# Exponentials turned by DMAs inside SBUF, and decay tiles spread from a table by VectorE, in a fused decay-attention and feed-forward kernel

## Chip, cores and metric

The kernel runs on one core of a Trainium2 chip. The metric is device time in microseconds of one execution; before the change it is 1072.73 us (median of 3 runs, 1070.98 to 1072.88). A core has TensorE (PE in the profile; its weight loads are PEld), VectorE (DVE), ScalarE (ACT), GpSimd (POOL) and SyncE (SP), which here issues nearly all DMAs. SBUF is the on-chip memory of 128 partitions, PSUM the matmul output with eight banks of 512 fp32 columns.

## The reference

For 8 batches of 8 heads, 576 positions and 64 dimensions, causal attention with a decay; its output, 4608 tokens of 512 features, goes through a feed-forward with a leaky slope per hidden unit.

```python
scores = scale * np.matmul(q, k.transpose(0, 1, 3, 2))
log_f = np.log(np.clip(f, 0.0001, 1.0))
cum = np.cumsum(log_f, axis=-1)
decay = cum[:, :, :, None] - cum[:, :, None, :]
causal = np.triu(np.ones((S, S), dtype=bool), k=1)
scores = np.where(causal, -1000000000.0, scores + decay)
scores = scores - np.max(scores, axis=-1, keepdims=True)
attn = np.exp(scores)
attn = attn / (np.sum(attn, axis=-1, keepdims=True) + 1e-09)
attn_out = np.matmul(attn, v)
...
h = x @ w_in
g = np.maximum(h, 0.0) + alpha * np.minimum(h, 0.0)
out = g @ w_out
```

The decay of the query's own position is the same for a whole row and drops out with the maximum, so only the keys' `cum` has to be added to the scores.

## The kernel before

**Work.** Two heads make a pair; pair n (0 to 31) is batch n // 4. `attention(n)` does one pair, `ffn1(b)` the first feed-forward product of batch b for 16 blocks of hidden units (`ffn1(8)` takes the last 64 positions of all batches), `ffn2(u)` the second one for a unit of 256 tokens. The first product stores its hidden values in DRAM (`hd`, line 807) and the second loads them again, as seven products of sums.

**Order.** Nothing is run in program order. Every step is an `op` of class `Plan` with an engine, an estimated duration, a key (smaller goes first), the steps that it depends on, and the buffers of `Ring`s that it holds. `Plan.run` simulates the engines and emits on each engine's queue the step that can start first, the smaller key among equals. DMAs go through one modelled channel (line 160). Attention of pair n has keys around 10 n, `ffn1` keys from 1e6, so the feed-forward fills what the attention leaves of TensorE. Each engine then works through its queue in order, and waits where something is not ready.

**One pair.** `load_n` (line 425) loads q and k (433, 434) and, from pair 4 on, splits each in two parts (ScalarE 472, GpSimd 473). It makes the decay tiles `Z` (two heads, all 128 partitions hold the same row of -8 cum) and `Zt` (for the tail): for pair 0 by a small matmul, for the others by DMAs from the DRAM row `c8`, broadcast to the partitions (443, 463). GpSimd adds the causal mask to their blocks (447 to 449, 464). The 576 queries are four tiles of 128 and a tail of 64 per head; the tail's two heads share 128 partitions. For each tile TensorE makes the scores (`stretch`, `tail`), VectorE adds the decay and takes the minimum (639, 541), and ScalarE takes the exponential in SBUF (508; tiles `es` and `e`).

P·V needs the exponentials with keys in the partitions. So TensorE transposes each block of 128 x 128 (`blocks`, 521; 677 for the last 64 keys of the tail), and ScalarE copies them from PSUM (517, tiles `eT`). For the fourth tile (i = 3) of pairs from `NX[0]` = 8 on another way is taken: the tile goes to DRAM (`ex`, 659), comes back in blocks of 32 partitions (`em`, 660), and VectorE transposes blocks of 32 x 32 (665). A reordered copy of v (`vs`, 497) goes with it. P·V (`prods_of`) is emitted with the third tile's scores of the next pair (`values`, `behind`); both heads run side by side on 64 columns each.

`quotients` and `fetch` bring the row sums through DRAM to a broadcast tile `ri` (598). `rest` multiplies (721) and splits the result into x (723, 725), in a ring of seven buffers, one per pair, which `ffn1` of that batch frees.

**Beside it.** `split64` (306 to 329) loads each of 16 blocks of `w_in` as 64-bit floats into two buffers `wr` (313) and turns them into two fp32 parts `wi` on ScalarE, VectorE and GpSimd; a work tile `wa` goes with it. `ffn1` takes a PSUM bank of ring `rH` for a block, twelve matmuls of 512 columns fill it (793), ScalarE and VectorE take it out (800 to 806) into one of four buffers `hs`. When the attention is done, its SBUF is given to the weights and buffers of `ffn2`.

Some lines that the steps go by:

```python
PC = ((0, 256), (256, S))
...
o_c8 = op("SP", 400, lambda: sy.dma_start(c8, ft()), -49, o_8, [bft], kb=147)
...
rx = Ring(Store([xx[:, 1024 * i : 1024 * i + 1024].rearrange("p (k q) -> p k q", k=2) for i in range(7)]))
...
for tiles in ((0, 1), (2,), (3,)) if n < NE else ((0, 1, 3), (2,)):
```

Of the kernel before, what the change touches and what calls it, by code (L numbers as in the profile page):

```python
# [29 lines left out]
NX = (8, B * NP)  # L30
# [53 lines left out]
class Plan:  # L84
# [30 lines left out]
    def run(self):  # L115
# [7 lines left out]
        while left:  # L123
# [63 lines left out]
def attention_moe(  # L187
    ctx: ExitStack,
    tc: tile.TileContext,
    qq: bass.AP,  # L190
    kk: bass.AP,
    vv: bass.AP,
    vs: bass.AP,
# [20 lines left out]
    ex = [dram.tile([2, 128, 512], F32, name=f"ex{i}") for i in range(2)]  # L214
# [32 lines left out]
    rrq = ring(sp, 2, [128, QW], F32, "rq")  # L247
    rrk = ring(sp, 2, [128, S], F32, "rk")
    rZ = Ring(Store([(sp.tile([128, 2, ZW], F32, name=f"Z{i}"), sp.tile([128, S], F32, name=f"Zt{i}")) for i in range(2)]))
    rvr = ring(sp, 2, [128, 5, 2, D], F32, "vr")  # L250
# [13 lines left out]
    rwr = ring(sp, 2, [128, 512], U64, "wr")  # L264
    rwa = ring(sp, 1, [128, 512], U32, "wa")
# [7 lines left out]
    wbf = sp.tile([128, 512], BF16, name="wbf")  # L273
    sel = sp.tile([9, 6, 128], F32, name="sel")
# [150 lines left out]
    def load_n(n, held):  # L425
# [4 lines left out]
        bq, bk, bZ = Buf(rrq), Buf(rrk), Buf(rZ)  # L430
        kq = -99 if first else -59 if n == 1 else kl
        dq = [] if first else [o_scan]
        l_q = op("SP", 450, lambda: sy.dma_start(bq.t, qq[b, p]), kq, dq, [bq], kb=320)
        l_k = op("SP", 450, lambda: sy.dma_start(bk.t, kk[b, p]), kq, dq, [bk], kb=288)
        Z, Zt = (lambda: bZ.t[0]), (lambda: bZ.t[1])
        rz = []
        for h in range(2):
            if first:
# [12 lines left out]
        if first:  # L451
# [13 lines left out]
        if n < NN:  # L465
            held += [bq, bk]
            return [l_q, l_k], rz, rt, bZ, [(lambda: bq.t, lambda: bk.t)]
# [3 lines left out]
        for hi, lo, raw, ld, w in ((Qh, Ql, bq, l_q, QW), (Kh, Kl, bk, l_k, S)):  # L471
            o1 = op("ACT", c_acs(w), lambda hi=hi, raw=raw: ac.activation(hi(), raw.t, AF.Copy), kc, [ld], [raw, bQ])  # L472
            o2 = op("POOL", c_po(w), lambda hi=hi, lo=lo, raw=raw: po.tensor_tensor(lo(), raw.t, hi().bitcast(F32), ALU.subtract), kc, [o1], [raw, bQ])  # L473
            out += [o1, o2]
# [3 lines left out]
    waiting, behind, later_x = [], [], []  # L478

    def attention(n):  # L480
# [9 lines left out]
        bv = Buf(rvr)  # L490
        l_v = op("SP", 400, lambda: sy.dma_start(bv.t, vv[b, p]), kl + 1, [o_scan], [bv], kb=320)
        nt_ = 3 if n >= NN else 4
        bT1, bT2 = [Buf(rT1) for _ in range(2)], [Buf(rT2) for _ in range(2)]
        b3, bT3, turned = Buf(re3), Buf(rT3), NX[0] <= n < NX[1]
        if turned:
            bm, bvs = Buf(rm3), Buf(rvs)
            l_s = op("SP", 400, lambda: sy.dma_start(bvs.t, vs[b, p]), kl + 12, [o_scan], [bvs], kb=256)
# [27 lines left out]

        def tail(st):

            bt = Buf(re)
            prev = None
            for g in range(2):  # L530
# [9 lines left out]
                def red(bS=bS, ks=ks, g=g):  # L540
                    ve.tensor_tensor_reduce(out=bt.t[:, ks], in0=bS.t[:, :288], in1=bZ.t[1][:, ks],  # L541
                                            scale=-0.125, scalar=lo()[:, 9:10] if g else 3.0e38, op0=ALU.add, op1=ALU.min,
                                            accum_out=lo()[:, 4:5] if g else lo()[:, 9:10])
# [16 lines left out]
        def quick(bR, r_, key):  # L560
# [11 lines left out]
            q_ = op("PE", 1400, prods, key, [r_, o_sel], bB + [bR])  # L572
            for c0, c1 in ((0, 512), (512, S)):
# [30 lines left out]
        def stretch(tiles, st):  # L604
# [16 lines left out]
            s_0.append(s)  # L621
            done(s)
# [4 lines left out]
        def tile(h, i, st, bS, s, c0):  # L627
# [4 lines left out]
            at = (lambda t: t[:, h]) if i == 3 else (lambda t: t)  # L632
# [21 lines left out]
            if i == 3 and turned:  # L654
                if h == 0:
                    return
                d = ex[n % 2]
                key = k0 + 7.8
                o_ = op("SP", 400, lambda: sy.dma_start(d.rearrange("h q k -> q h k"), b3.t), key, [be[0][3][1], nm], [b3], kb=512)
                got = [op("SP", 400, lambda k=k: sy.dma_start(  # L660
                    bm.t[32 * k : 32 * k + 32], d[:, :, 128 * k : 128 * k + 128].rearrange("h (a c) s -> c (h a) s", c=32)),
                    key + 0.1, [o_], [bm], kb=128) for k in range(4)]
                for h_ in range(2):
                    def turn(h_=h_):
                        ve.transpose(bT3.t[:, h_].rearrange("p s (a c) -> p a s c", a=4),
                                     bm.t[:, 4 * h_ : 4 * h_ + 4].rearrange("p a (s r) -> p a s r", r=32))

                    e3.append(op("DVE", c_tr(512), turn, k0 + 13.5, got, [bm, bT3]))
                return
            if i >= 2:  # L670
# [3 lines left out]
                def tr2():  # L674
                    blocks(bT.t, 0, at(b1.t), range(i + 1))
                    if last:
                        pe.transpose(bT.t[0:64, 384:512], bt.t[:, 512:S], ident)  # L677

                t = op("PE", (i + 1 + last) * 109, tr2, st + 0.3, [nm, o_id] + ([nt] if last else []), [bT, b1] + ([bt] if last else []))
                to, tb = ((lambda: bT3.t[:, h]), bT3) if i == 3 else ((lambda: bT2[h].t[:, 0 : i + 1, 0:128]), bT2[h])  # L680
# [6 lines left out]
        def prods_of(r, out):  # L687

            def pv():
                both = []  # L690
                o = out()
                for h in range(2):
                    e1_, e2_ = bT1[h].t, bT2[h].t
                    if r == 0:
                        both.append([(0, 0, 256, e1_[:, 0:256]), (1, 128, 256, e1_[:, 256:384])])
                    else:
                        both.append([(j, 0, 128, e2_[:, j, 0:128]) for j in range(3)]
# [118 lines left out]
    for fc in range(NF):  # L816
        load_w_in(fc)
# [294 lines left out]
```

## Time and profile before

| What | Value |
| --- | --- |
| Time, median of 3 runs | 1072.73 us |
| Profiled execution: device time, span of the trace | 1073.41 us, 1071.6 us |
| Mean granted TensorE clock | 0.992 |
| DMA traffic | 202.15 MB, 189 GB/s |
| First feed-forward product, 1728 matmuls of 512 columns | 428.4 us busy on TensorE |
| Decay tiles by DMA (443, 463) | 62 loads of 256 KB, 62 of 144 KB |
| Round trip of the fourth tile (659, 660) | 24 stores of 512 KB, 96 loads of 128 KB |

The profile is one execution, recorded by the hardware. In a row of a group stand the line, the engine, the operation, the tile written and the tiles read, the shapes and the count; behind the bar the busy time in all and the mean of one in ns; then the engine's idle time just before and what ended it. In the timeline a row starts with its start and its length, both in us. "Busy" of TensorE counts matmuls from issue to the end that the profile models, and these overlap, so rows that follow each other closely are timed by the distance of their starts.

### The profile page before, as it was taken

The page shows a single profiled execution, that of the slowest core. Times are in us where ns is not written, and L with a number is a line of the kernel's source. Part 1 is how long each engine was busy: PE and PEld are TensorE (multiplying, and loading weights), DVE is VectorE, ACT ScalarE, POOL GpSimd, SP SyncE. Part 2 cuts the span into 40 slices and gives each one's busy share as a digit, 9 for nine tenths or more (in the row PEclk, how much of TensorE's full clock was granted, in tenths as well). Part 3 has the DMA queues.
Part 4 walks back from the last instruction along what each step waited for, and adds up shares of the span by engine and source line. Part 5 has one row for each costly group of instructions (what it writes and reads, how often), then busy time and mean ns, then how long its engine had stood idle before and what let it go on. Part 6 is the DMA issues. An engine that isn't in the chain of part 4 may idle for free.

```text
span 1071.6 us, 22543 instructions
## 1 busy us (share of the span) xinstructions
PE 1054.9 (98%) x8132; PEld 916.7 (86%) x8132; DVE 738.6 (69%) x1680; ACT 675.0 (63%) x1590; POOL 280.5 (26%) x407
## 2 busy tenths in 40 slices
PE   8889989999999999999999999999999999999998
PEld 5678867888888888888788888899999999999998
DVE  6788864555544545545544599779988898989994
ACT  6879877786766766667655375656454554646551
POOL 6578574553433434344221000000000000000000
PEclk9989999999999999999999999999999999999999
DMA  6967778987887986886763666464444443444411
GB/s 181 268 194 235 225 217 232 271 264 238 253 237 214 259 241 203 242 247 212 215 198 129 204 214 225 167 199 139 136 126 132 137 137 120 138 130 126 140 60 40
DMA packets 152441, 202.15 MB, mean 189 GB/s; under 512 B 18930, under 2 KB 89481, under 8 KB 152329
## 3 DMA queue, kind: packets, MB, share of 16 engines
q1 hardware_dynamic: 152041, 200.51, 61.3%
q8 instruction: 64, 1.05, 0.4%
q14 instruction: 48, 0.39, 0.1%
q10 hardware_dynamic: 288, 0.20, 0.1%
HBM read 139.55 MB, written 61.11 MB: 187 GB/s over the span
## 4 chain that ended last, share of the span: by engine, by line
PE 92%; DMA 2%; POOL 2%; DVE 1%; issue 1%; ACT 1%; SPq 0%; DVEq 0%; POOLq 0%
PE bank L332 86%; PE bank L521 5%; DMA Z<-c 2%; PE bank L392 1%; POOL Z L447 1%; DMA wr<-in_w_in_dram 0%; POOL wi L328 0%; POOL Z L448 0%; PE bank L677 0%; DVE eT L516 0%; DVE wa L322 0%; POOL Z L449 0%; ACT e L508 0%; POOL Ql L473 0%; POOL Kl L473 0%
## 5 line engine op out<-in xcount | busy, mean ns | idle before, releaser
L332 PE MATMUL bank<-xx,wi 128*128 128x512 f32 x1728 | 428.4, 397 | 2.3 <-ACT wi L327 1.8
L332 PEld LDWEIGHTS bank<-xx,wi 128*128 128x128 f32 x1728 | 314.4, 188 | 68.7 <-issue 4.8
L805 DVE SCALAR_TENSOR_TENSOR hs<-bank,sa,hs 128x512 f32<-128x512 f32 x96 | 71.2, 743 | 109.9 <-ACT hs L803 109.8
L332 PE MATMUL bank<-wot,xx 128*128 128x256 f32 x1008 | 123.9, 283 | 0.0
L332 PE MATMUL bank<-wi,xx 128*128 128x256 f32 x1008 | 123.9, 283 | 0.0
L332 PEld LDWEIGHTS bank<-wot,xx 128*128 128x128 f32 x1008 | 122.3, 192 | 0.0
L332 PEld LDWEIGHTS bank<-wi,xx 128*128 128x128 f32 x1008 | 122.3, 192 | 0.0
L508 ACT ACTIVATE e<-e,st 128x512 f32<-128x512 f32 (+2 forms) x160 | 109.2, 685 | 4.2 <-DVE st L541 2.0
L803 ACT ACTIVATE hs<-bank,ab 128x512 f32<-128x512 f32 x96 | 66.0, 688 | 63.4 <-PE bank L332 62.6
L517 ACT ACTIVATE eT<-bank 128x384 f32<-128x384 f32 (+2 forms) x192 | 83.3, 461 | 34.7 <-PE bank L332 20.1
L725 POOL TENSOR_TENSOR xx<-xs,xx 128x256 fp32r<-128x256 f32 x64 | 49.0, 783 | 136.6 <-ACT xx L723 136.4
L473 POOL TENSOR_TENSOR Ql<-rq,Qh 128x640 fp32r<-128x640 f32 x28 | 45.1, 1611 | 137.8 <-ACT Qh L472 89.7
L332 PE MATMUL bank<-eT,vr 128*64 128x128 f32 (+2 forms) x1408 | 80.0, 263 | 0.2 <-DVE eT L516 0.2
L332 PEld LDWEIGHTS bank<-eT,vr 128*64 128x64 f32 x1408 | 63.9, 138 | 14.1 <-issue 7.1
L447 POOL TENSOR_TENSOR Z<-Z,tri 128x384 f32<-128x384 f32 x64 | 60.0, 945 | 45.5 <-DMA Z<-c 31.2
L999 ACT ACTIVATE xx<-gx 128x1024 fp32r<-128x1024 f32 x48 | 50.8, 1058 | 30.8 <-PE bank L332 15.1
L521 PEld LDWEIGHTS bank<-ident,e 128*128 128x128 f32 x384 | 46.9, 146 | 20.5 <-issue 5.3
L521 PE MATMUL bank<-ident,e 128*128 128x128 f32 x384 | 62.2, 287 | 1.9 <-DVE st L639 1.6
L1002 DVE TENSOR_TENSOR xx<-gx,xx 128x1024 fp32r<-128x1024 f32 x48 | 58.6, 1220 | 7.4 <-ACT xx L999 7.4
L332 PE MATMUL bank<-wi,gh 128*128 128x256 f32 x504 | 62.4, 283 | 0.0
L332 PE MATMUL bank<-wot,gh 128*128 128x256 f32 x504 | 62.4, 283 | 0.0
L332 PEld LDWEIGHTS bank<-wot,gh 128*128 128x128 f32 x504 | 61.4, 192 | 0.1
(140 smaller groups left out, 1777.6 us busy)
## 6 DMA issues: line engine op xcount, KB each, us to landing
hd<-hs SPq DMA_DIRECT2D x144, 256.0 KB
wx<-hd SPq DMA_DIRECT2D x47, 512.0 KB
Z<-c SPq DMA_DIRECT2D x62, 256.0 KB
hr<-hd SPq DMA_DIRECT2D x25, 512.0 KB
ex<-e SPq DMA_DIRECT2D x24, 512.0 KB
em<-ex SPq DMA_DIRECT2D x96, 128.0 KB
rq<-in_qq_dram SPq DMA_DIRECT2D x32, 320.0 KB
vr<-in_vv_dram SPq DMA_DIRECT2D x32, 320.0 KB
```

Of the source, the lines that this page charges most:

```text
L332: pe.matmul(o, lhsT, rhs, start=start, stop=stop)
L392: op("PE", 800, lambda: [pe.matmul(bw.t, wbf[:, 0:128], wbf, start=True, stop=True) for _ in range(3)], -200, [o_wbf], [bw])
L447: m1 = op("POOL", c_po(128 * 3), lambda z4=z4: po.tensor_tensor(z4()[:, 6:9], z4()[:, 0:3], tb(3), ALU.add), kc + 0.1, got + [o_mask], [bZ])
L473: o2 = op("POOL", c_po(w), lambda hi=hi, lo=lo, raw=raw: po.tensor_tensor(lo(), raw.t, hi().bitcast(F32), ALU.subtract), kc, [o1], [raw, bQ])
L508: ex = op("ACT", c_exp(w), lambda: ac.activation(at(bt.t)[:, :w], at(bt.t)[:, :w], AF.Exp, bias=lo()[:, col : col + 1], scale=-1.0, accum_ ...
L517: return op("ACT", c_act(w), lambda: ac.activation(dst(), src(), AF.Copy), key, deps, [bank] + bufs)
L521: pe.transpose(t[:, c : c + 128], src[:, 128 * j : 128 * j + 128], ident)
L725: xl = op("POOL", c_po(256), lambda r=r, t0=t0: po.tensor_tensor(bx.t[:, 1, t0 : t0 + 256], bxs[r].t[:, 0:256], bx.t[:, 0, t0 : t0 + 256]. ...
L803: cp = op("ACT", c_act(512), lambda bh=bh, bs=bs, fc=fc: ac.activation(bs.t, bh.t, AF.Relu, scale=ab[:, fc : fc + 1]), -1000, [last, o_sg] ...
L805: cp = op("DVE", c_dve(512), lambda bh=bh, bs=bs, fc=fc: ve.scalar_tensor_tensor(bs.t, bh.t, sa[:, fc : fc + 1], bs.t, ALU.mult, ALU.add), ...
L999: his.append(op("ACT", c_acs(128 * GW * (j1 - j0)), lambda j0=j0, j1=j1, src=src, o_=o_: ac.activation(o_(0, j0, j1), src(), AF.Copy), key ...
L1002: rdy.append(op("DVE", c_dve(128 * GW * (j1 - j0)), lambda j0=j0, j1=j1, src=src, o_=o_: ve.tensor_tensor(o_(1, j0, j1), src(), o_(0, j0, ...
```

## The change

Seven things change together.

- From pair 9 on (`NX[0]` 9 instead of 8) the fourth tile's and now also the tail's exponentials are moved by 16 DMAs straight from SBUF to SBUF (32 partitions, three groups of 128 columns each), not by way of DRAM. VectorE turns three groups instead of two. Only the last 64 keys of the tail are still transposed by TensorE. P·V takes the 128 columns of the fourth tile and the 64 of the tail in one product (`bT3` holds 192 columns per head and key block), so that a pair's second product chain has 8 products per head instead of 12. Pair 8 is done as the earlier pairs are.
- From pair 10 (`NZ`) on the decay tiles are no longer loaded. Once all of `w_in` is split, `c8` is loaded once as 64 rows (`cl`), VectorE transposes it in blocks to a table (`cq`, `cq2`) with heads in the columns, six DMAs copy it to the other three groups of 32 partitions, and GpSimd picks the tail's columns (`ct`). For a pair VectorE then reads a column of the table 32 times over and transposes, which fills `Z` and `Zt`.
- q and k share one buffer, and from pair 4 (`NQ`) on they come as one load. Turned pairs load v and its reordered copy as one tensor `vt`.
- The landing place `em`, the rows `cl` and the table `cq` lie in the buffers of the `w_in` split (`wr`, `wa`), so the first turn has to wait for the table. `wbf`, the operand of the matmuls at the very start, lies there too.
- The buffers `eT2` are regrouped after pair 8's P·V: two of two heads each, and a second one for `e3`.
- The planner's channel reckons with 220 instead of 280 GB/s for DMAs that it starts before 90 us.
- `ex`, `vs` and their rings are gone.

```diff
-NX = (8, B * NP)
+FAR = 90.0
+NX = (9, B * NP)
+NZ = 1+9
+NQ = 4
...
-                self.chan = max(self.chan, s + 1.4) + o.kb / 280.0
+                self.chan = max(self.chan, s + 1.4) + o.kb / (220.0 if s < FAR else 280.0)
...
-    rT2 = ring(sp, 4, [128, 4, 192], F32, "eT2_")
-    rT3 = ring(sp, 1, [128, 2, 4, 128], F32, "eT3_")
-    rm3 = ring(sp, 1, [128, 8, 128], F32, "em")
-    rvs = ring(sp, 1, [128, 4, 2, D], F32, "vs")
+    t2s = sp.tile([128, 4, 800], F32, name="eT2_")
+    rT2 = Ring(Store([t2s[:, i, 0:768].rearrange("p (j q) -> p j q", q=192) for i in range(4)]))
+    rT2b = Ring(Store([]))
+    rT3 = ring(sp, 1, [128, 4, 384], F32, "eT3_")
+    wr = sp.tile([128, 1280], U64, name="wr")
+    wf = wr.bitcast(F32)
+    rm3 = Ring(Store([]))
+    em = wf[:, 0:1536].rearrange("p (k s) -> p k s", s=128)
+    cl = wf[0 : B * H, 0:S]
+    cq = wf[:, 1536:2560].rearrange("p (s g) -> p s g", g=B * H)
...
-    re3 = ring(sp, 1, [128, 2, 512], F32, "e3_")
+    re3 = ring(sp, 1, [128, 1024 + S], F32, "e3_")
...
+        spread = NZ <= n
+        if spread:
+            def rows_of(src, k):
+                return src.rearrange("p s (h o) -> p h s o", o=1).broadcast_to([128, k, src.shape[1], 32])
+
+            zz = op("DVE", c_tr(1024), lambda: ve.transpose(
+                Z()[:, :, 0:512].rearrange("p h (s c) -> p h s c", c=32), rows_of(cq[:, 0:16, 2 * n : 2 * n + 2], 2)), kl + 4, [o_cq], [bZ])
+            zt = op("DVE", c_tr(S), lambda: ve.transpose(
+                Zt().rearrange("p (s c) -> p s c", c=32), rows_of(ct[:, :, n : n + 1], 1)[:, 0]), kl + 4.1, o_ct, [bZ])
...
-            bt = Buf(re)
+            bt = b3 if turned else Buf(re)
...
-            nt = expo(bt, S, 4, st + 0.6, [prev])
+            nt = expo(bt, S, 4, st + 0.6, [prev], tail_of)
+            if turned:
+                return bt, nt
...
-                o_ = op("SP", 400, lambda: sy.dma_start(d.rearrange("h q k -> q h k"), b3.t), key, [be[0][3][1], nm], [b3], kb=512)
-                got = [op("SP", 400, lambda k=k: sy.dma_start(
-                    bm.t[32 * k : 32 * k + 32], d[:, :, 128 * k : 128 * k + 128].rearrange("h (a c) s -> c (h a) s", c=32)),
-                    key + 0.1, [o_], [bm], kb=128) for k in range(4)]
...
+                src = lambda a, k: b3.t[32 * a : 32 * a + 32, 0:1536].rearrange("p (g s) -> p g s", g=3)[:, :, 128 * k : 128 * k + 128]
+                dst = lambda a, k: bm.t[32 * k : 32 * k + 32].rearrange("p (g a) s -> p g a s", a=4)[:, :, a]
+                got = [op("SP", 400, lambda a=a, k=k: sy.dma_start(dst(a, k), src(a, k)), key + (4 * a + k) / 100,
+                          [be[0][3][1], nm, nt], [b3, bm], kb=64) for a in range(4) for k in range(4)]
+                for g in range(3):
...
+                            for h_ in range(2):
+                                ve.transpose(bT3.t[:, :, 192 * h_ + 128 : 192 * h_ + 192].rearrange("p s (a c) -> p a s c", a=2),
+                                             bm.t[:, 8 + 2 * h_ : 10 + 2 * h_].rearrange("p a (s r) -> p a s r", r=32))
...
+                        if turned:
+                            both.append(head + [(j + 4, 128, 320, t3[:, j]) for j in range(3)] + [(3, 256, 320, bT4.t[:, 64 * h : 64 * h + 64])]
+                                        + [(7, 128, 320, t3[:, 3])])
...
+    o_cl = op("SP", 400, lambda: sy.dma_start(cl, c8), kc_, [o_c8] + [o for v in w_ready.values() for o in v], kb=147)
...
+            ve.transpose(cq[0:32, :, 32 * g : 32 * g + 32], src[:, 0:16])
+            ve.transpose(cq2[0:32, :, 32 * g : 32 * g + 32], src[:, 16:18])
...
+    o_qc = [op("SP", 400, lambda a=a, c=c: sy.dma_start(c[32 * a : 32 * a + 32], c[0:32]), kc_ + 2, o_tc, kb=128) for a in range(1, 4) for c in (cq, cq2)]
+    o_cq = op("-", 0, lambda: rm3.store.items.append(em) or rm3.store.free.append((plan.t, 0)), 0, o_tc + o_qc)
...
+    o_ct = [op("POOL", c_po(S) + 60, lambda h=h: sides(h), kc_ + 3, [o_cq]) for h in range(2)]
```

More of the change, by code (lines that the diff above doesn't have):

```diff
@@ L263, in attention_moe @@
     rR = ring(sp, 2, [18, 128], F32, "R")
-    rwr = ring(sp, 2, [128, 512], U64, "wr")
-    rwa = ring(sp, 1, [128, 512], U32, "wa")
+    rwr = Ring(Store([wr[:, 512 * i : 512 * i + 512] for i in range(2)]))
+    rwa = Ring(Store([wf[:, 2048:2560].bitcast(U32)]))
     ident = sp.tile([128, 128], F32, name="ident")
@@ L450, in load_n @@
             rz.append([m1, m2, m3])
-        if first:
+        if spread:
+            tz = [zt]
+        elif first:
             bz2 = [Buf(rH), Buf(rH)]
@@ L621, in stretch @@
             s_0.append(s)
+            if after:
+                value_ops.append(s)
             done(s)
@@ L696, in pv @@
                     else:
[L697 to L700 removed]
+                        t3 = bT3.t[:, :, 192 * h : 192 * h + 192]
+                        head = [(j, 0, 128, e2_[:, j]) for j in range(3)]
+                        if turned:
+                            both.append(head + [(j + 4, 128, 320, t3[:, j]) for j in range(3)] + [(3, 256, 320, bT4.t[:, 64 * h : 64 * h + 64])]
+                                        + [(7, 128, 320, t3[:, 3])])
+                        else:
+                            both.append(head + [(j, 128, 256, t3[:, j, 0:128]) for j in range(4)]
+                                        + [(j, 256, 320, bT2[h].t[:, j, 128:192]) for j in range(4)] + [(4, 256, 320, bT4.t[:, 64 * h : 64 * h + 64])])
+                first, last = (((0, 3), (2, 7)) if turned else ((0, 3, 7), (2, 6, 11))) if r else ((0,), (1,))
                 for c, pair in enumerate(zip(*both)):
                     for h, (j, q0, q1, m) in enumerate(pair):
[L703 removed]
+                        mm(o[64 * h : 64 * h + 64, q0:q1], bv.t[:, j, h], m, c in first, c in last)
             return pv
@@ L813, in attention_moe @@
     o_sg = op("DVE", 800, signs, 0.6, [o_al, s_0[-1]])
-    for n in range(1, B * NP):
+    for n in range(1, NX[0]):
         attention(n)
```

115 lines of the change are left out of this document (68 added, 47 removed).

## The prediction

> **What bounds the kernel now.** I read the page's head and slices first, then busy time by stage, then the waits.
>
> ```profile
> span 1071.6 us, 22543 instructions
> ...
> PE 1054.9 (98%) x8132; PEld 916.7 (86%) x8132; DVE 738.6 (69%) x1680; ACT 675.0 (63%) x1590; POOL 280.5 (26%) x407
> ```
>
> TensorE is busy 98% of the span, but busy counts matmuls that overlap, so the question is where it ever runs dry. One call of the windows view gives that by stage (the stretch and its length, then busy time and count of PE, PEld, DVE, ACT and POOL, then TensorE's granted clock, DMA share, GB/s):
>
> ```profile
> 48.00:74.00 26.00, 20.07 (x138) 15.58 (x139) 22.48 (x55) 18.60 (x52) 18.87 (x27) 0.74 0.66 198
> 74.00:146.00 72.00, 72.00 (x613) 58.86 (x612) 53.76 (x130) 63.62 (x173) 52.10 (x62) 1.00 0.71 221
> 146.00:162.00 16.00, 12.74 (x63) 9.32 (x63) 11.30 (x26) 10.68 (x29) 11.24 (x14) 1.00 0.83 252
> 162.00:581.00 419.00, 418.78 (x3358) 338.82 (x3357) 210.39 (x633) 290.11 (x803) 167.51 (x237) 1.00 0.79 231
> 581.00:705.00 124.00, 124.00 (x592) 102.62 (x591) 87.30 (x149) 68.79 (x106) 3.92 (x4) 1.00 0.58 194
> 705.00:1071.60 366.60, 362.71 (x3023) 362.50 (x3021) 320.17 (x587) 188.16 (x328) 0.00 (x0) 1.00 0.40 125
> ```
>
> From 162 us on TensorE lacks work for 0.22 us of 419, then for nothing until the closing drain. Before 162 us it does run dry, in two places: 5.93 us of 48 to 74 and 3.26 us of 146 to 162. So a microsecond of TensorE work removed behind 162 us should come off the end, and one removed ahead of it need not. The changed pairs (9 to 31) run in the stage 162 to 581: the first `em` load, pair 8's, is issued at 154.6 us (row of line 660 below).
>
> That the attention could be fed faster would bring nothing there. The list of waits (total, times, longest) and two rows of the timeline show why. GpSimd's x split (line 725) waits on the rounding before it, which waits for a free buffer of the x ring, and the buffers come back only when a feed-forward batch ends:
>
> ```profile
> POOL xx L725 <- ACT xx L723: 136.4, 26, 24.8
> ...
> POOL Z L447 <- DMA Z<-c: 31.2, 23, 5.7
> ...
> DVE eT L665 <- DMA em<-ex: 17.8, 8, 3.7
> ```
> ```profile
> 252.09 2.92 POOL L725 TENSOR_TENSOR xx<-xs,xx 128x256 fp32r<-128x256 f32 x4 [0.51 <-ACT xx L723]
> ```
> ```profile
> 253.63 2.55 PE L332 MATMUL bank<-xx,wi 128*128 128x512 f32 x10
> ```
>
> The x of the next batch's last pair is made in the microsecond in which that batch's matmuls follow (252.09, then 253.63). The attention is held back by the feed-forward, not the other way. This is why I cost the removed transfers at nothing, below.
>
> **Removed from TensorE.** The tail's exponentials lose their four 128-wide transposes in each of 23 pairs. Prices stand in the chain of work (first row: six transposes; second: four behind a P·V) and in TensorE's timeline:
>
> ```profile
> 192.99 0.66 PE bank L521 x6
> ...
> 197.28 0.59 PE bank L521 x4
> ```
> ```profile
> 180.98 0.88 PE L332 MATMUL bank<-eT,vr 128*64 128x128 f32 x12
> 181.68 1.04 PE L332 MATMUL bank<-eT,vs 128*64 128x128 f32 x16
> 182.56 1.40 PE L332 MATMUL bank<-eT,vr 128*64 128x64 f32 x28
> 183.89 1.65 PE L332 MATMUL bank<-xx,wi 128*128 128x512 f32 x6
> ```
>
> 0.66 / 6 = 0.11 us a transpose, so 4 x 0.11 = 0.44 us a pair and 23 x 0.44 = 10.1 us. The 0.59 us row holds 0.15 us more, a switch from the matmuls ahead. Some other group will pay that switch, so I count none of it; at most it is 23 x 0.15 = 3.4 us.
>
> P·V goes from 12 products per head to 8 by joining 128- and 64-wide ones into 192-wide ones. The columns stay the same (7 x 128 + 5 x 64 = 1216 = 3 x 128 + 4 x 192 + 64), only instructions go: 16 of the 56 rows of a pair. The 16 `vs` rows take from 181.68 to 182.56, 0.055 us each at two heads and two passes; the whole P·V takes 2.91 us. The saving lies between nothing (time goes by columns) and 0.2 us a pair (16 rows of a fixed 0.0125). I take 0.05, near the column end, since the rows so far follow the columns: 1.2 us, range 0 to 4.6.
>
> **Added to TensorE.** Pair 8 is no longer turned by DMA: eight transposes, 8 x 0.11 = 0.9 us. They fall at 146 to 162, where TensorE has idle time, so 0 to 0.9; I count 0.9. Sum: 10.1 + 1.2 - 0.9 = **10.4 us less**.
>
> **Other engines, costed at nothing.** VectorE gains two spreads and a third turn per pair. ScalarE loses two copies of 256.
>
> ```profile
> L665 DVE STREAM_TRANSPOSE eT<-em 128x512 f32<-128x512 f32 x48 | 32.0, 693 | 42.5 <-DMA em<-ex 17.8 <-DMA rq<-in_qq_dram 7.3 <-PE bank L332 6.5
> ...
> L517 ACT ACTIVATE eT<-bank 128x256 f32<-128x256 f32 x56 | 18.5, 385 | 4.9 <-PE bank L521 4.9
> ```
>
> In proportion to 693 ns for 512: 1024 columns 1.39, 576 columns 0.78, the third turn (2 x 256) 0.69, so 2.9 us a pair and about 63 us in 22 to 23 pairs. VectorE is busy 210 of 419 us in that stage, 273 after. ScalarE drops by 2 x 0.385 x 23 = 18 us. The table costs once: a load, four small transposes, six copies by DMA and two GpSimd copies, which no row shows. Its length lies between the 5.3 us of a Z load (168.48 to 173.83, below) and some 15 us, three such steps in a row; I take the longer. It stands in pair 10's path only, while batch 1's matmuls lie ready for TensorE, and that batch ends at 253 us, where the next one needs pair 10. Nothing, then; without that cover up to 15 us.
>
> What goes of the DMA: 800 KB of decay tiles a pair and the 1024 KB round trip through DRAM, against 768 KB from SBUF to SBUF. Today's waits on them (31.2 and 17.8 us in the list above) are off TensorE's path, since it idles 0.22 us in that stage. The loads that are joined (q with k, v with its reordered copy) only drop issues.
>
> ```profile
> 168.48 0.88 SPq L443 DMA_DIRECT2D Z<-c  x2
> ```
> ```profile
> 159.82 1.61 POOL L328 TENSOR_TENSOR wi<-wa,wi 128x256 fp32r<-128x256 f32 x2
> ...
> 173.83 1.80 POOL L447 TENSOR_TENSOR Z<-Z,tri 128x384 f32<-128x384 f32 x2 [1.13 <-DMA Z<-c]
> ```
>
> Pair 10's Z is asked for at 168.48 and used at 173.83. The table can start only when the last w_in part is split (159.82 + 1.61 = 161.4), so it is about as late. What waits for it: GpSimd's additions of the mask (447 to 449), with the Q and K splits (473) queued behind them on GpSimd, and pair 9's turn, whose landing place is now part of the w_in buffers; both have the cover of batch 1.
>
> Now the sixteen DMAs that replace one store and four loads. SyncE issues every one, and feed-forward stores (line 807) queue behind them:
>
> ```profile
> L660 SPq DMA_DIRECT2D em<-ex x96: 303/449/1250, 154.6 to 575.1; - x96
> ```
> ```profile
> 418.24 0.39 SPq L659 DMA_DIRECT2D ex<-e  x1
> ...
> 423.62 2.18 SPq L660 DMA_DIRECT2D em<-ex  x4
> ```
> ```profile
> 431.48 0.71 DVE L665 STREAM_TRANSPOSE eT<-em 128x512 f32<-128x512 f32 x1 [2.71 <-DMA em<-ex]
> ```
>
> Today the way from store to turn takes 431.48 - 418.24 = 13.2 us, 6 of it from the last load's issue to its use. Sixteen issues of 0.449 take 7.2 us, and with the same 6 us the way is again 13.2. There is one hop instead of two, and no Z load ahead in the queue. The turn is as punctual as now, and VectorE's wait there (2.71 us in this row, 3.7 at most) has cost TensorE nothing.
>
> **The number.** The profiled execution took 1073.41 us (span 1071.6 and 1.8 around it), 0.7 above the median of 1072.73. 1073.41 - 10.4 = 1063.0 in its frame, **1062.3 us** against the median.
>
> **Rivals.**
> 1. *The early stage moves too.* The planner now reckons with 220 instead of 280 GB/s before 90 us, and q and k come as one load from pair 4, so the order before 162 us is another. What a gap costs is in finer windows:
>
> ```profile
> 48.00:50.00 2.00, 0.00 (x0) 0.00 (x0) 2.00 (x3) 0.86 (x2) 1.16 (x2) 1.00 0.93 218
> 50.00:52.00 2.00, 1.43 (x5) 1.01 (x7) 1.97 (x9) 2.00 (x7) 1.74 (x3) 0.58 1.09 350
> 52.00:54.00 2.00, 2.00 (x7) 0.59 (x4) 0.52 (x3) 2.00 (x7) 2.00 (x4) 0.50 0.72 254
> 54.00:56.00 2.00, 2.00 (x11) 1.96 (x10) 1.97 (x7) 1.95 (x7) 2.00 (x5) 0.50 0.74 202
> 56.00:58.00 2.00, 2.00 (x21) 1.63 (x21) 1.97 (x4) 2.00 (x5) 0.87 (x2) 0.71 0.35 124
> ```
> 2.6 us of idleness are followed by some 7 us at about half clock: 1.43 x 0.42 + 1.0 + 1.0 + 0.58 = 3.2 us more, so 5.8 a gap. The Trainium skill's page "TensorE: Matmul & The Clock Gate", section "HAM oscillation — how this bites in real kernels", allows gaps of up to about 3.4 us before the clock falls. The row disagrees: here one of 2.6 us was enough. If half of what the two early places lose (5.9 + 3.3 idle and 0.26 x 20.07 = 5.2 of clock, 14.4 in all) goes, 1062.3 - 7.2 = 1055.1: chance 0.15. If one more such gap comes, 1062.3 + 5.8 = 1068.1: 0.10. No row favours a sign, so the forecast takes nothing.
> 2. *Slower: the turns hold up VectorE.* VectorE runs in order, and behind a turn that waits stands the feed-forward's line 805, which frees TensorE's banks. Two banks are kept for the feed-forward, each filled by twelve matmuls in some 2.75 us (ten take 2.55 with the last one's tail, row 253.63), so TensorE starves when VectorE waits longer than 5.5 us. If the sixteen land late enough for waits of 7 us, each of 23 pairs loses 1.5 us: 1062.3 + 34.5 = 1096.8. It decides the sign from (10.4 + 2.1) / 23 = 0.54 us a pair, a wait of 6.0 us. For it: 3.7 us has been seen. Against: the reckoning of 13.2 us. Chance 0.11. The Trainium skill's page "DMA: Bandwidth & Descriptors", section "Measured (HBM→SBUF, 128 partitions, SWDGE, issued from GpSimd)", says to batch to 1 MiB and calls transfers under 64 KB descriptor-dominated; with its fixed 2.0 us (section "Anatomy of one DMA — SWDGE (gpsimd) path") in series, 16 DMAs would be an estimated 32 us a pair. The row of four loads issued in 2.18 us speaks against series, so this adds nothing to the 0.11.
> 3. *It does not do what it says.* The transposes go, but P·V waits for the later of three turns about as long (0.45 us a pair): 1062.3 + 10.4 = 1072.7, chance 0.06.
>
> **Chances and range.** The forecast has 0.58. Its own bounds are 10.1 - 0.9 = 9.2 less and 10.1 + 3.4 + 4.6 = 18.1 less, 1063.5 to 1054.6. With both early cases the range is 1054 to 1070 and leaves out 0.17. A measurement of this kernel tells about 0.2% (2.1 us) from no change: faster 0.58 + 0.15 + 0.10 = 0.83, within 0.06, slower 0.11.
>
> **What would show it.** Transposes of `e` at line 521's counterpart fall from 384 to 384 - 92 + 8 = 300. TensorE idles under 1 us between 170 us and the start of the output stage. The last w_in split on GpSimd stays near 160 us (far earlier or later is rival 1). VectorE's waits before the turns stay under 4 us. I am wrong if TensorE shows idle time inside that stage, or if the feed-forward's matmuls there get slower.

## Result: slower by 3.2%, and the profile after

The changed kernel takes 1105.55 us (median of 4 runs, 1104.85 to 1108.42) against 1072.63 us for the kernel before in the same runs (1070.98 to 1072.88): a ratio of 1.0315, 95% interval 1.0294 to 1.0336. The forecast was 1062.3 us, with a range to 1070.

Busy times and chain from the page of the changed kernel (the chain's shares are by engine):

```profile
PE 1061.5 (96%) x7680; PEld 914.4 (83%) x7680; DVE 796.7 (72%) x1772; ACT 662.8 (60%) x1546; POOL 282.6 (26%) x411
...
PE 71%; SPq 11%; DVE 7%; DMA 7%; issue 2%; ACT 1%; POOL 0%; DVEq 0%
```

TensorE has 452 matmuls fewer (8132 to 7680). SyncE's own issuing of DMAs (SPq) now makes up 11% of the chain that ends last. The stages, in the same windows as in the prediction:

```profile
48.00:74.00 26.00, 19.61 (x141) 15.25 (x140) 24.79 (x52) 17.11 (x48) 22.50 (x27) 0.80 0.72 202
...
146.00:162.00 16.00, 16.00 (x144) 12.88 (x141) 10.86 (x32) 14.82 (x42) 7.61 (x8) 1.00 0.58 172
162.00:581.00 419.00, 390.89 (x2662) 307.49 (x2662) 251.83 (x679) 256.26 (x703) 167.93 (x240) 0.97 0.57 160
```

The stage of the changed pairs, 162 to 581 us, had 0.22 us of idle TensorE before. Now it has 419 - 390.89 = 28.1 us, and the granted clock is 0.97 instead of 1.00 (3% of 390.89 = 11.7 us, good to about 2 us, since the clock is printed with two digits). Together that is some 40 of the 43.3 us by which the run missed the forecast. The 16 us ahead of it are full. DMA share fell from 0.79 to 0.57, so the DMA engines are not what is short.

The waits (total, times, longest) name where it starts:

```profile
POOL Z L468 <- DVE Z L452: 104.2, 15, 12.5
...
DVE eT L700 <- DMA wr<-eT__112: 55.7, 10, 7.8
DVE eT L700 <- DMA wr<-e: 32.0, 10, 4.5
...
PE bank L341 <- DVE hs L848: 13.1, 7, 4.0
...
PE bank L341 <- DVE eT L703: 5.3, 4, 2.5
```

Line 700 is the turn (VectorE's transposes of what the sixteen DMAs bring; line 703 is its third group), line 848 the old line 805 (it frees TensorE's banks), line 341 the matmuls. VectorE waits for the turn's DMAs 20 times, up to 7.8 us (3.7 before). Of TensorE's 28.1 idle us, 13.1 end with line 848 and 5.3 with the third group of the turn, which P·V needs; most of the others end with further steps of VectorE. The first row shown, GpSimd waiting for the spread, is large too; the run with the DRAM route below keeps the spread, and there GpSimd waits 92.6 us for it while TensorE has no idle time in this stage, so that wait by itself costs nothing.

The rows of the sixteen DMAs (lengths of one issue: shortest, median, longest; the `wr` they write holds the landing place):

```profile
L694 SPq DMA_DIRECT2D wr<-e x192: 590/597/1557, 170.3 to 615.0; - x192
L694 SPq DMA_DIRECT2D wr<-eT__112 x176: 585/597/1810, 187.3 to 588.5; - x176
```

One such stall, first in SyncE's timeline (start, length), then VectorE's, then TensorE's:

```profile
295.11 2.20 SPq L694 DMA_DIRECT2D wr<-eT__112  x3
297.42 1.52 SPq L630 DMA_DIRECT2D ri<-rd  x1
...
300.86 2.58 SPq L694 DMA_DIRECT2D wr<-eT__112  x4
303.53 0.53 SPq L515 DMA_DIRECT2D vr<-in_vt_dram  x1
304.11 5.73 SPq L694 DMA_DIRECT2D wr<-eT__112  x9
```
```profile
311.32 1.30 DVE L700 STREAM_TRANSPOSE eT<-wr 128x512 f32<-128x512 f32 x2 [4.16 <-DMA wr<-eT__112]
312.54 0.71 DVE L848 SCALAR_TENSOR_TENSOR hs<-bank,sa,hs 128x512 f32<-128x512 f32 x1
```
```profile
308.55 1.64 PE L341 MATMUL bank<-xx,wi 128*128 128x512 f32 x6
313.31 0.55 PE L341 MATMUL bank<-Kh,Qh 64*128 64x384 f32 x2 [3.12 <-DVE hs L848]
```

Read it from top to bottom. The sixteen issues (3 + 4 + 9) take 2.20 + 2.58 + 5.73 = 10.5 us, and 4.2 us of other issues and pauses lie between them, so the last ends at 309.84. The turn starts at 311.32, 16.2 us after the first issue. This is one of the longer ways: the median of the 23 turned pairs is 14.2 us from the first issue to the turn (12.9 to 17.4). VectorE has stood still for 4.16 us, then does the first two groups, then line 848 at 312.54. TensorE's last matmuls began at 308.55 and ended about 310.2; the next begin at 313.31. The granted clock falls behind such a gap:

```profile
314.00:316.00 2.00, 1.46 (x14) 0.96 (x12) 1.83 (x7) 0.98 (x3) 0.00 (x0) 0.50 0.85 124
```

### The profile page after: what moved, and what is told of

Its sections match the earlier page's. It is cut to its first block, busy times and chain, and to the rows that moved or that the text cites. A ratio compares the mean times of both kernels' runs of the same rounds, so it can differ in the third digit from the quotient of the medians.

```text
span 1103.7 us, 21705 instructions
## 1 busy us (share of the span) xinstructions
PE 1061.5 (96%) x7680; PEld 914.4 (83%) x7680; DVE 796.7 (72%) x1772; ACT 662.8 (60%) x1546; POOL 282.6 (26%) x411
## 4 chain that ended last, share of the span: by engine, by line
PE 71%; SPq 11%; DVE 7%; DMA 7%; issue 2%; ACT 1%; POOL 0%; DVEq 0%
PE bank L341 67%; SPq L694 9%; PE bank L548 3%; DMA wr<-eT__112 2%; DMA ri<-rd 1%; DVE eT L700 1%; DMA rd<-R 1%; SPq L630 1%; DMA vr<-in_vt_dram 1%; DVE hs L848 1%; DMA wr<-e 1%; DVE eT L703 1%; PE bank L401 1%; SPq L850 1%; DVE xs L764 1%
## 5 line engine op out<-in xcount | busy, mean ns | idle before, releaser
L535 ACT ACTIVATE e<-e,st 128x384 f32<-128x384 f32 (+2 forms) x127 | 84.9, 671 | 35.5 <-DVE st L570 33.3
L700 DVE STREAM_TRANSPOSE eT<-wr 128x512 f32<-128x512 f32 x46 | 30.2, 692 | 101.0 <-DMA wr<-eT__112 55.7
L341 PE MATMUL bank<-eT,vr 128*64 128x192 f32 (+3 forms) x896 | 78.0, 322 | 5.3 <-DVE eT L703 5.3
L341 PEld LDWEIGHTS bank<-eT,vr 128*64 128x64 f32 x896 | 61.3, 147 | 17.0 <-DVE eT L703 6.7
L341 PE MATMUL bank<-Kh,Qh 64*128 64x128 f32 (+1 forms) x280 | 62.1, 365 | 11.1 <-DVE hs L848 9.1
L496 POOL TENSOR_TENSOR Ql<-rqk,Qh 128x640 fp32r<-128x640 f32 x28 | 45.1, 1611 | 65.3 <-ACT Qh L495 56.3
L535 ACT ACTIVATE es<-es,st 128x256 f32<-128x256 f32 (+1 forms) x128 | 56.7, 444 | 8.5 <-DVE st L673 8.5
```

Of the source, the lines that this page charges most:

```text
L341: pe.matmul(o, lhsT, rhs, start=start, stop=stop)
L535: ex = op("ACT", c_exp(w), lambda: ac.activation(at(bt.t)[:, :w], at(bt.t)[:, :w], AF.Exp, bias=lo()[:, col : col + 1], scale=-1.0, accum_ ...
L700: ve.transpose(o, bm.t[:, 4 * g : 4 * g + 4].rearrange("p a (s r) -> p a s r", r=32))
```

## Experiments

**Theories.** A: the planner books 400 ns for each of the sixteen DMAs, but one takes about 645 ns from start to start (2.58 us for four), so it puts the turns too early in VectorE's queue; the loss is order. C: SyncE cannot issue sixteen such DMAs per pair in time beside its others (16 x 0.645 = 10.3 us of the 18 us that a pair has, 419 us for 23 pairs); the loss is its queue. B: the spreads of the decay tiles load VectorE too much. Each run stands beside a kernel before on the same chip.

| Run | Time, us (runs) | Ratio to before, 95% interval |
| --- | --- | --- |
| e1_plan_cost | 1086.22 (4) | 1.0138, 1.0100 to 1.0175 |
| e2_dram_route | 1058.38 (4) | 0.9879, 0.9847 to 0.9910 |
| e3_no_spread | 1145.45 (1) | |
| e4_dst_runs | 1105.58 (1) | |
| e5_two_queues | 1075.95 (1) | |
| e6_dram_no_spread | 1059.46 (4) | 0.9883, 0.9859 to 0.9908 |
| e8_far280 | 1060.70 (4) | 0.9893, 0.9866 to 0.9919 |
| e9_probe | 1075.80 (1) | |
| e10_dummies | 1088.69 (4) | 1.0140, 1.0108 to 1.0172 |
| e11_plan_late | 1103.46 (4) | 1.0287, 1.0259 to 1.0314 |

The kernel before took 1071.54 us (median) beside the first four, 1072.80 beside e5 to e9 and 1073.01 beside the last two.

### e1_plan_cost: the right price in the plan

```diff
-                got = [op("SP", 400, lambda a=a, k=k: sy.dma_start(dst(a, k), src(a, k)), key + (4 * a + k) / 100,
+                got = [op("SP", 645, lambda a=a, k=k: sy.dma_start(dst(a, k), src(a, k)), key + (4 * a + k) / 100,
```

> The kernel after the change, with one number changed: the planner reckons 645 ns for the issue of each of the sixteen DMAs (as the profile of the changed kernel shows, 597 ns and some 50 between two) instead of 400. The work is the same, only the order on the queues may differ. Theory A (SyncE issues the sixteen slower than the planner believes, so that the turns stand too early in VectorE's queue and hold up the feed-forward's steps behind them): VectorE's waits before the turns fall from 88 us to under 30, TensorE's idle time in the attention stage nearly goes, 1060 to 1075 us. Theory B (VectorE itself has too much to do with 2.9 us more a pair): stays at 1095 to 1110. Theory C (SyncE's queue is the limit whatever the order: 16 x 0.645 = 10.3 us of some 18 a pair): 1085 to 1105.

Only the order of instructions changes. 19.3 us of the loss go, but the waits at the turn (windows, then waits) do not:

```profile
162.00:581.00 419.00, 405.18 (x2769) 323.17 (x2770) 257.85 (x689) 260.91 (x711) 170.18 (x242) 0.99 0.58 166
```
```profile
DVE eT L700 <- DMA wr<-eT__112: 57.3, 11, 8.6
DVE eT L700 <- DMA wr<-e: 29.0, 10, 4.6
```

86.3 us of waiting against 87.7, now placed where TensorE suffers half as much: 13.8 us idle instead of 28.1. A holds for part of the loss, but its mark (waits under 30) does not come, and the time lies in the range that C gave. What TensorE waits for has changed too: mostly for the third group of the turn itself, at P·V, and no longer for its banks:

```profile
PE bank L341 <- DVE eT L703: 8.5, 7, 4.9
...
PE bank L341 <- DVE hs L848: 5.2, 3, 1.9
```

### e2_dram_route: the same three groups through DRAM

```diff
...
-                got = [op("SP", 400, lambda a=a, k=k: sy.dma_start(dst(a, k), src(a, k)), key + (4 * a + k) / 100,
-                          [be[0][3][1], nm, nt], [b3, bm], kb=64) for a in range(4) for k in range(4)]
+                d = ex[n % 2]
+                o_ = op("SP", 400, lambda: sy.dma_start(d.rearrange("g q k -> q g k"), b3.t[:, 0:1536].rearrange("p (g s) -> p g s", g=3)), key, [be[0][3][1], nm, nt], [b3], kb=768)
+                got = [op("SP", 400, lambda k=k: sy.dma_start(
+                    bm.t[32 * k : 32 * k + 32], d[:, :, 128 * k : 128 * k + 128].rearrange("g (a c) s -> c (g a) s", c=32)),
+                    key + 0.1, [o_], [bm], kb=192) for k in range(4)]
```

> The kernel after the change, but the three groups (fourth tile and tail) go by one store to DRAM and four loads of 192 KB, as the fourth tile did before; decay tiles still come from the table. Five issues a pair instead of sixteen. Theory A and theory C: about 1062 us (the 10.4 us of TensorE work gone and no stalls), 1056 to 1070. Theory B: 1095 to 1110, since VectorE has the same work.

Five DMAs per pair instead of sixteen, everything else of the change kept. This is faster than both kernels: 0.9879 of the time before, with an interval that leaves out 1. Its windows and its waits:

```profile
162.00:581.00 419.00, 419.00 (x2939) 335.67 (x2936) 272.79 (x727) 278.21 (x756) 171.71 (x247) 1.00 0.76 217
```
```profile
DVE eT L702 <- DMA wr<-ex: 26.9, 21, 2.8
```

More bytes move (DMA share 0.76 against 0.57), yet TensorE is never idle here and VectorE's longest wait at the turn is 2.8 us. The whole loss hangs on the sixteen DMAs.

### e3_no_spread: direct DMAs, decay tiles loaded as before

```diff
-NZ = 1+9
+NZ = 99
...
-    kc_ = NS * NZ - 28
+    kc_ = 72
```

> The kernel after the change, but all decay tiles are loaded by broadcasting DMA as before (the table is still made, since the landing place waits for it, but not used). VectorE is spared 2.0 us a pair, SyncE issues four more loads a pair. Theory A and theory C: no better than 1105, rather 1105 to 1130. Theory B: 1062 to 1075.

All decay tiles are loaded again; the table is still made. If the spreads were too much for VectorE, this had to be faster. It is 40 us slower, and 15 us beyond the range that A and C gave (one run):

```profile
162.00:581.00 419.00, 373.16 (x2421) 294.42 (x2420) 187.46 (x570) 233.54 (x636) 144.51 (x205) 0.95 0.63 183
```
```profile
DVE eT L700 <- DMA hd<-hs: 58.7, 6, 11.1
```

VectorE has least to do and TensorE starves most, with waits at the turn up to 11.1 us (for these six the profile names a store, not a DMA of the turn, as what ended them). B falls. Four more loads per pair on SyncE make it worse, which speaks for C.

### e4_dst_runs: longer runs in the landing place

```diff
-dst = lambda a, k: bm.t[32 * k : 32 * k + 32].rearrange("p (g a) s -> p g a s", a=4)[:, :, a]
+dst = lambda a, k: bm.t[32 * k : 32 * k + 32].rearrange("p (a g) s -> p a g s", g=3)[:, a]
...
```

The turns read by the matching pattern. Each DMA now writes one run of 1536 bytes per partition instead of three of 512.

> The kernel after the change, with the landing place laid out so that each DMA writes one run of 1536 B per partition instead of three of 512 B (it still reads three runs of 512 B); the same bytes, the same order of work. It asks what the 597 ns of an issue depends on. If on the writes' runs: the issue falls towards 450 ns and theories A and C give 1075 to 1095 us. If on the reads or on the number of DMAs alone: 590 to 600 ns and 1100 to 1110 us. Theory B expects 1100 to 1110 either way.

```profile
L694 SPq DMA_DIRECT2D wr<-e x192: 586/597/1588, 167.8 to 615.1; - x192
```

The issue takes 597 ns as before, and the time is the same, 1105.58 us. The price does not come from the runs written.

### e5_two_queues: half of the sixteen issued by ScalarE

```diff
...
+                        if a < 2:
+                            sp_.append(op("SP", 645, lambda a=a, k=k: sy.dma_start(dst(a, k), src(a, k)), key + (4 * a + k) / 100,
+                                          [be[0][3][1], nm, nt], [b3, bm], kb=64))
+                        else:
+                            ac_.append(op("ACT", 600, lambda a=a, k=k: ac.dma_start(dst(a, k), src(a, k)), key + (4 * a + k) / 100,
+                                          [be[0][3][1], nm, nt], [b3, bm]))
+                got = sp_ + [op("-", 2400, lambda: None, key, ac_)]
```

> Eight of the sixteen DMAs stay on SyncE (planned at 645 ns each), the other eight are issued from ScalarE's queue. If SyncE's own queue is the limit (16 x 0.645 = 10.3 us of the 18 us that a pair has), SyncE's issues fall from 16 to 8 per pair, VectorE's waits at line 700 shrink from 86 us (with the corrected plan) to under 40, and the time comes to 1060 to 1075 us. If only the order in VectorE's queue mattered, it stays at 1080 to 1090 like the run with the corrected plan. If the issues cost ScalarE as much (8 x 0.6 = 4.8 us per pair of its 60 per cent load), waits of VectorE and TensorE on ScalarE show, and the time is over 1086.

1075.95 us, 1 us above the range that C gave (one run), and 10.3 us better than e1_plan_cost. The waits at the turn all but vanish:

```profile
DVE eT L708 <- DMA wr<-eT__112: 6.4, 4, 2.8
DVE eT L708 <- DMA wr<-e: 5.7, 4, 2.2
```
```profile
303.78 0.62 ACT L535 ACTIVATE e<-e,st 128x384 f32<-128x384 f32 x1 [4.81 <-DMA wr<-eT__112]
```

12.1 us against 86.3. The price has moved: ScalarE's exponential in the second fence (its timeline) starts after 4.81 idle us, the last 3.8 of them spent on four of its own DMA issues. TensorE idles 10.7 us in the stage from 162 to 581 us, and 8.8 of these end with ScalarE's exponentials. The Trainium skill's page "DMA: Bandwidth & Descriptors", section "Issuing engines are not separate DMA queues", says that issuing from several engines only saves the issuing engine's time, usually small beside the transfer. Here the sum of that time was the large one: 0.6 us an issue, 10.3 us for sixteen in a row, against 2.0 us from an issue to its landing in the changed kernel (median of line 694).

### e6_dram_no_spread: the DRAM route without the spreads

e2_dram_route with the two edits of e3_no_spread.

> The three groups go through DRAM and all decay tiles are loaded by DMA as before the change, so TensorE's removed transposes stand alone. By the prediction's sum for TensorE 1061 to 1063 us. If the table is needed to leave SyncE and the DMAs room (as it was with the direct DMAs, where leaving it out cost 40 us), 1070 us or more, with VectorE's waits at the turn over 4 us. If the table itself costs time through VectorE, 1050 to 1057, below the run with table and DRAM route (1058.4).

```profile
162.00:581.00 419.00, 418.57 (x2934) 334.79 (x2933) 234.51 (x680) 276.91 (x753) 167.95 (x238) 1.00 0.90 257
```

1059.46 us, not to be told from e2_dram_route, and between two of the ranges named. TensorE is full even at a DMA share of 0.90. So with the DRAM route the table is worth nothing that can be measured. What is gained is 0.92 to 1.41% of 1072.80, that is 9.9 to 15.1 us. It holds TensorE's removed work and also the 3.26 us that TensorE idled from 146 to 162 us before the change: this run has none there.

### e8_far280: the planner's channel as before

```diff
-FAR = 90.0
+FAR = 0.0
```

On e2_dram_route; the model of the channel is 280 GB/s from the start again.

> The DRAM route with the table, and the planner's channel at 280 GB/s from the start instead of 220 in its first 90 us. If that edit is worth nothing by itself, 1056 to 1061 us as the DRAM route with it. If it carries part of what the DRAM route gained, the first feed-forward batch of the second batch starts later than 166 us and the time is 1062 or more.

1060.70 us; its interval overlaps that of e2_dram_route widely. This edit carries nothing of note.

### e9_probe: the price of an issue by itself

e2_dram_route with 28 DMAs added at its end, when SyncE has nothing else to do; so its whole time isn't compared.

> The DRAM route with 28 more DMAs at the very end, seven shapes four times each, when SyncE has nothing else to do: 32 partitions of three runs of 128 columns from SBUF to SBUF (the change's own shape); 32 partitions of one run of 384; 128 partitions of one run of 384; the first shape from SBUF to DRAM and back; the second shape from SBUF to DRAM and back. If the issue time goes by the number of descriptors, the first shape (96 runs) takes about three times the second (32), and the third as much as four of the second. If it goes by the route, all SBUF to SBUF shapes take about 0.59 us and those with DRAM 0.3 to 0.46. If it is load on SyncE in the attention stage that made 0.59, all are shorter here.

In the order of the seven shapes (SBUF to SBUF 32 partitions x 3 runs, 32 x 1, 128 x 1; SBUF to DRAM x 3 runs, x 1; DRAM to SBUF x 3 runs, x 1):

```profile
L1150 SPq DMA_DIRECT2D xx<-xx x4: 585/618/736, 1054.3 to 1056.6; - x4
L1152 SPq DMA_DIRECT2D xx<-xx x4: 581/588/589, 1057.2 to 1059.1; - x4
L1154 SPq DMA_DIRECT2D xx<-xx x4: 537/552/559, 1059.8 to 1061.7; - x4
L1156 SPq DMA_DIRECT2D pr<-xx x4: 597/606/622, 1062.4 to 1064.3; - x4
L1158 SPq DMA_DIRECT2D pr<-xx x4: 419/422/592, 1065.0 to 1066.5; - x4
L1160 SPq DMA_DIRECT2D xx<-pr x4: 578/594/595, 1067.0 to 1068.9; - x4
L1162 SPq DMA_DIRECT2D xx<-pr x4: 419/420/582, 1069.5 to 1071.1; - x4
```

The change's own shape takes 618 ns on an idle queue, so 597 ns is the price of the instruction and not of a crowded SyncE. It doesn't follow the number of runs (96 take 618, 32 take 588, 128 take 552), and not the route alone (three runs from or to DRAM take 594 and 606, one run 420 and 422). None of the three expected patterns fits; what sets the price stays open.

### e10_dummies: SyncE's load without the way of the turn

```diff
...
+                for k in range(11):
+                    op("SP", 645, lambda k=k: sy.dma_start(
+                        dx[k].rearrange("p (g s) -> p g s", g=2), wf[0:32, 1536:2560].rearrange("p (g s) -> p g s", g=2)[:, :, 0:128]),
+                        key + 0.2 + k / 100, got[:1] + [o_], [], kb=32)
```

On e2_dram_route: eleven extra DMAs per pair whose result nobody reads.

> The DRAM route with five DMAs per pair on the way of the turn, and eleven more per pair on SyncE behind them, small ones from the table to a place in DRAM that nobody reads, planned at 645 ns each: SyncE again issues sixteen DMAs per pair, but nobody waits for eleven of them. If SyncE's occupied time as such delays everything else that it issues (theory C), the time goes to 1075 to 1090, near that of the sixteen real ones with the corrected plan (1086.2). If it matters only that the turn stands behind sixteen issues in a row, it stays at 1056 to 1064.

1088.69 us, 30.3 us over the same kernel without them and in the range that C gave. The stage, the waits, and a stretch of SyncE's timeline:

```profile
162.00:581.00 419.00, 401.18 (x2702) 316.76 (x2700) 248.72 (x678) 256.53 (x705) 166.84 (x241) 1.00 0.78 218
```
```profile
DVE eT L707 <- DMA wr<-ex: 62.5, 17, 5.4
...
DVE eT L707 <- DMA dx<-wr: 24.7, 5, 6.2
```
```profile
236.79 5.48 SPq L700 DMA_DIRECT2D dx<-wr  x6
...
244.74 1.87 SPq L700 DMA_DIRECT2D dx<-wr  x3
246.71 0.53 SPq L695 DMA_DIRECT2D ex<-e  x1
...
251.09 1.86 SPq L696 DMA_DIRECT2D wr<-ex  x4
```

Dummies hold up what stands behind them, here the next pair's store at 246.71: its last exponential had ended on ScalarE at 234.1. The waits at the turn come back (26.9 to 87.2 us in the rows shown), and TensorE idles 17.8 us, 8.0 of them until the third group of a turn. From store to turn the way isn't longer: its median over the 23 pairs is 12.4 us in both kernels (11.3 for this pair, whose turn starts at 258.04). It all starts later. From the end of a pair's last exponential to its store, a median of 0.2 us passes in e2_dram_route and 8.9 us here (timelines of ScalarE and SyncE). The lengths of SyncE's issue rows between 162 and 581 us, added up from its timeline (a row of several issues holds the pauses between them), come to about 49% of that stage in e2_dram_route, 60% in the kernel before, 82% here, 85% in the changed kernel and 86% in e1_plan_cost. Two caveats: at 5 of these 22 waits the profile names a dummy as the releaser, so the turn may wait by a count that the dummies share; that is 24.7 of the 87.2 us. And each dummy follows the landing of a load of the turn, for which SyncE itself stood still 14.1 us in that stage (28 waits), so not all of the loss is issuing.

### e11_plan_late: the turns planned later still

```diff
+                got = [op("-", 2400, lambda: None, key, got)]
```

On e1_plan_cost: 2.4 us more between the DMAs and the turns in the plan.

> All sixteen direct DMAs on SyncE, planned at 645 ns, and the three turns planned another 2.4 us later, so that they stand further back in VectorE's queue. If the rest of the loss (1086.2 against 1058.4) is still order, VectorE's wait at the turn shrinks from 86 us to under 45 and the time comes to 1062 to 1075. If the queue of SyncE itself is the limit, the time stays at 1080 to 1092, and the waits only move to P.V or to the loads of q, k and v.

1103.46 us, beyond either theory's range. The stage, and the waits of the turn (line 701 here) and of TensorE for the next batch's x (line 767):

```profile
162.00:581.00 419.00, 394.98 (x2599) 310.39 (x2599) 246.27 (x650) 248.50 (x674) 159.66 (x232) 0.97 0.55 159
```
```profile
DVE eT L701 <- DMA wr<-eT__112: 0.9, 1, 0.9
...
PE bank L341 <- ACT xx L767: 17.2, 6, 4.0
```

The turn hardly waits any more, and TensorE starves for another reason: a pair's chain has become so long that the attention falls behind the feed-forward, and a batch's matmuls wait for x. So the rest of the loss isn't got back by a later place for the turn. In kind that is what C expects (the wait moves); that it costs 17 us more than e1_plan_cost, C did not expect.

## Why the prediction was wrong, by its own steps

**The step that failed** is the term for the sixteen DMAs: "Sixteen issues of 0.449 take 7.2 us, and with the same 6 us the way is again 13.2 ... The turn is as punctual as now". The size of the issue was taken from the loads of line 660, another shape. It is 0.597, 0.645 from start to start, so 10.3 us a pair, and 4.2 us of other issues and pauses lay between them in the stall shown. The landing was overpriced (2.0 us, not 6), which hides the error in the sum: the way is 16.2 us in that stall and 14.2 in the median of the 23 pairs, against the 13.2 that the step gave. That one to three us of way is not the whole cost, and that the sum came out so near is luck: two errors offset each other. The step asked only how long the turn's way is, and left out that SyncE spends those 10.3 us on nothing else. e10_dummies puts such a load at some 30 us with the way from store to turn as short as in e2_dram_route.

**Rival 2** had the mechanism: VectorE in order, the waiting turn, line 805 behind it, TensorE's banks. It had 0.11. Its 1096.8 us was 9 us short. Its point of decision, a wait of 6.0 us, was too high: in the stall shown a wait of 4.16 us cost TensorE 3.12. (Two banks take 5.9 us, not the 5.5 reckoned: in the timeline of the kernel before, twelve matmuls run from 253.63 to the next row at 256.56.) VectorE stopped at 311.32 - 4.16 = 307.16 and TensorE had work until about 310.2, so 3 us of work stood ready, not the full two banks, and the two groups of the turn (1.30 us) pass before line 848 as well. It also had no term for the clock, about 11.7 us here. Rival 3's wait, P·V behind the last turn, came too: 5.3 us of TensorE's idle time here and 8.5 of 13.8 in e1_plan_cost.

**The plan's order** was in no step. The planner books 400 ns for each issue, and the right number alone is worth 19.3 us.

**TensorE's sum holds.** 10.4 us less (bounds 9.2 to 18.1) was forecast; with the DRAM route the whole gain is 9.9 to 15.1 (e6_dram_no_spread), up to 3.3 of it from the early stage. One P·V takes 2.87 us in e2_dram_route (184.53 to 187.40) instead of 2.91: 0.04 a pair, where 0.05 was taken. Transposes of `e` fell from 384 to 300 as counted. This and the prices on VectorE are in the groups of the changed kernel (busy in all, mean ns):

```profile
L548 PE MATMUL bank<-ident,e 128*128 128x128 f32 x300 | 49.3, 290 | 3.8 <-ACT e L535 2.1 <-DVE st L673 1.6
...
L452 DVE STREAM_TRANSPOSE Z<-wr 128x1024 f32<-128x1024 f32 x22 | 27.4, 1244 | 0.7
...
L703 DVE STREAM_TRANSPOSE eT<-wr 128x256 f32<-128x256 f32 x46 | 16.9, 406 | 0.0
L454 DVE STREAM_TRANSPOSE Zt<-sel 128x576 f32<-128x576 f32 x22 | 16.7, 761 | 0.0
```

A pair costs VectorE 1.24 + 0.76 + 2 x 0.41 = 2.8 us; 2.9 was forecast, and that it costs nothing holds (e2_dram_route, e6_dram_no_spread).

**The early stage** (rival 1): 146 to 162 us has no idle TensorE now (3.26 before) and 48 to 74 us is nearly as it was. So it moved, in idle time by under half of the 7.2 us that the rival took; e8_far280 finds nothing in the channel's number, and what else filled it is not shown. **The table** hid behind batch 1, as argued: with it, e2_dram_route has no idle TensorE from 146 to 581 us. **The removed loads** are worth nothing with five DMAs a pair, as forecast, but not with sixteen: there they buy 40 us (e3_no_spread), which fits SyncE as the limit.

**The marks.** VectorE's waits were to "stay under 4 us" and went up to 7.8; idle TensorE "inside that stage" was named as the sign of error, and 28.1 us of it came. The other sign, slower matmuls of the feed-forward, did not: 398 ns in the mean against 397.

What is left open: how the 27.8 us between e1_plan_cost and e2_dram_route split between SyncE's load and the longer chain before the turn, since e10_dummies puts back mostly the first and loses as much (in e1_plan_cost the median way is 15.6 us, in e2_dram_route 12.4); where the rest of e10_dummies' 30.3 us goes beside the 17.8 us of idle TensorE; and how much of the 17.6 us that issues on two queues still leave is ScalarE's own issuing (e5_two_queues, one run).

## What to carry to other kernels

Cost a DMA twice: its way from issue to use, and the time it takes from the engine that issues it, which all other DMAs of that queue pay. Splitting one store and four loads into sixteen small copies removed bytes that were free and added issue time that was not. Where a planner orders the work, give each new kind of instruction its measured price before judging the idea.

## What the runs showed of the hardware

A copy of 48 KB from SBUF to SBUF takes SyncE 0.59 to 0.62 us to issue even when it has nothing else to do (first two rows of e9_probe), and the third row's copy, four times as large, takes less, 0.55. Twelve of the 768 KB stores of e2_dram_route are issued in 0.37 us (its line 694), so bytes do not set the price. The other eleven, of the same shape but from the second of two buffers, take 0.53 us, so the shape does not set it alone either; what does is open:

```profile
L694 SPq DMA_DIRECT2D ex<-e x12: 370/371/386, 159.0 to 555.2; - x12
L694 SPq DMA_DIRECT2D ex<-eT__114 x11: 378/532/541, 186.1 to 529.8; - x11
```

TensorE's granted clock fell to 0.50 behind an idle time of 3.12 us (result above), as it did behind one of 2.62 us in the kernel before (47.95 to 50.57).
